# Moving a filling unit's last sums, its denominators and the cut of the V transfers around two layer changes

## The chip, the cores and the metric

The kernel runs on one core of one Trainium2 chip. The metric is the device time of one execution in microseconds (us). The kernel before was timed three times: 2504.41, 2506.2 and 2507.76 us, so its median is 2506.2 us.

## The reference, cut to what matters

Four layers run one after another on an activation `x` of two batch rows with 512 channels: attention, token mixer, attention, token mixer. Each is added to its input.

```python
q = (x @ wq).reshape(B, Sq, Hq, Dh).transpose(0, 2, 1, 3)      # Hq = 32, Dh = 128
k = jnp.repeat(k_cache, 4, axis=1)                             # 8 kv heads, 32768 keys
v = jnp.repeat(v_cache, 4, axis=1)
p = softmax(einsum("bhqd,bhkd->bhqk", q, k) * Dh ** -0.5)
o = einsum("bhqk,bhkd->bhqd", p, v)
att = o.transpose(0, 2, 1, 3).reshape(B, Sq, Hq * Dh) @ wo

x = x + att(layernorm(x))
x = x + mixer(layernorm(x))    # layernorm, outer product with w1 (1792), + b1, gelu, times w2, + b2
x = x + att(layernorm(x))      # the same K and V caches again
x = x + mixer(layernorm(x))
```

Both attention layers read the whole K and V caches, 16 pairs of (batch row, kv head) with 16 MB of K and 16 MB of V each, all in float32. Each layer reads them from HBM once, 1064 MB in all with the weights, but for some cells that are kept between the layers, as told below.

## The kernel before, in words

**Units and steps.** A unit is `(layer, b, h)`: one attention layer, one batch row, one kv head with its four query heads. A unit has a K phase and a V phase. Each phase reads 64 cells; a cell is 128 partitions by 512 floats, 256 KB. Four cells are one step, so a phase has 16 steps in two halves. A K step is four matmuls into the tile `scores` (`k_step`, L335), a V step four matmuls into the tile `acc` (`v_step`, L388). The class `Order` writes out the order of all steps by hand: the K phase of a unit, then the V phase of the unit before it, and so on.

**The transfers.** One tile `mem` of 106 cells holds everything that comes from HBM. `plan_loads` decides, when the program is built, for each transfer how many cells it takes (32, 24, 16, 8 or 4, unless `Order.cut` prescribes a size), where in `mem` they lie, and after which step they are free. It reckons with its own prices, with the PE time that each hook announces (`us=`) among them, so a hook that is announced elsewhere can shift sizes and places of all later transfers. All transfers go through one queue, that of SyncE (SP, L823 for K and V, L816 for weights): it waits until the cells' last reader on TensorE is done, issues, and goes to the next; a transfer whose cells are not free holds up all behind it.

**The hooks.** Work beside the steps is hung on steps with `at(step, function, ...)` and issued behind that step in the order in which it was hung there. For a unit these are: `max_1` and `max_2` (the maximum of the scores), `turn_scores` (DVE transposes the scores, L365) and `exponentials` (ACT, L370) for each half, `denominators` (L410 to L413: sum the exponentials over the partitions, take the reciprocal `rl`), `take_out` (L419, DVE copies `acc` to the one buffer of the tile `row`), `out_1` (L427 on TensorE, the unit's heads as columns, then L442 on DVE divides them) and `out_2` (L451, the heads times `wo`, added into `rows`).

**The layer changes.** After the first attention layer the two batch rows change to the next layer one after the other. For each there are three units, `changes = ((x, fill, y), ...)`: `x` is the last unit of its batch row in layer 0, `y` the first of the same row in layer 1 (the same kv head as `x`, so all 64 V cells and 10 K cells of `x` are kept for `y`), and `fill` is a unit of the other batch row whose V phase runs while the mixer of `x`'s row is computed. So the order at a change is: V of `x`, V of `fill`, K of `y`, V of `y`. In the V phase of `fill` the hooks carry the chain of the change, one or two pieces behind each step: `out_1` and `out_2` of `x`, `take_rows`, `mix_2` (layer norm), seven pairs of Gelu tiles (`hidden_tiles`, L511 and L527), `take_rows`, `change_0` to `change_3`, at whose end the query of `y` stands in `qz` (L321). The V transfers of `fill` are cut to four cells and go through four places in `mem`; the K transfers of `y` are cut to four cells as well.

Before the change, the second half of V of `x` is cut to 16, 8, 4 and 4 cells (`TAPER`), V of the unit ahead of the first `x`, `before[-1]`, is not cut by hand, `out_1` of `fill` stands behind the first step of K of `y` and `out_2` behind the second, and its `denominators` behind the tenth step of its own V phase, which is behind the Gelu tiles:

```python
at(v0 - 1 if u == order.last else v_mid + 2, denominators, u, us=0.4)
...
late = 0 if u == order.v_before[order.last] else 1
at(v_end + late, out_1, u, us=1.2)
at(v_end + 2 * late, out_2, u, us=2.0)
...
e = v_end
at(e, out_1, u, us=1.9)
at(e + 1, out_2, u, us=2.0)
```

The last four lines are for a unit that ends its batch row in a layer, as `x` does: `e` is the end of its V phase, and all hooks of the change count from it.

Of the kernel before, what the change touches and what calls it, by code (L numbers as in the profile page):

```python
# [15 lines left out]
HALF = 32  # L16
# [24 lines left out]
class Order:  # L41


    def __init__(self, heads):
        far, f, s = list(range(heads - 2)), heads - 2, heads - 1
        self.steps = []
        self.pairs = []
        before = [(0, b, h) for h in far for b in (0, 1)] + [(0, 0, f)]
        x0, fill0, y0 = (0, 0, s), (0, 1, f), (1, 0, s)
        x1, fill1, y1, n = (0, 1, s), (1, 0, f), (1, 1, s), (1, 1, f)  # L50
        after = [(1, b, h) for h in far[:1:-1] for b in (0, 1)] + [(1, b, h) for b in (0, 1) for h in far[1::-1]]
        for i, u in enumerate(before):
            self.k(u)
            if i:
                self.v(before[i - 1])
        self.k(x0), self.v(before[-1]), self.k(fill0), self.v(x0), self.v(fill0)
        self.k(y0), self.v(y0), self.k(x1), self.k(fill1), self.v(x1), self.v(fill1)
        self.k(y1), self.v(y1), self.k(n)
        prev = n
        for u in after:  # L60
            self.k(u), self.v(prev)
            prev = u
        self.v(prev)
        self.last = prev
        self.changes = ((x0, fill0, y0), (x1, fill1, y1))
        self.units = before + [x0, fill0, y0, x1, fill1, y1, n] + after
        self.first, self.end = {}, {}
        for p, (kind, u, g) in enumerate(self.steps):
            self.first.setdefault((kind, u), p)
            self.end[kind, u, g // HALF] = p  # L70
        byv = sorted(self.units, key=lambda u: self.first["V", u])
        self.v_before = {u: byv[i - 1] if i else None for i, u in enumerate(byv)}
        self.last_of = {
            (layer, b): max((u for u in self.units if u[:2] == (layer, b)), key=lambda u: self.end["V", u, 1])
            for layer in (0, 1)
            for b in (0, 1)
        }
        self.first_of = {
            (layer, b): min((u for u in self.units if u[:2] == (layer, b)), key=lambda u: self.end["V", u, 1])
            for layer in (0, 1)  # L80
            for b in (0, 1)
        }
        self.kept = {}
        for x, _, y in self.changes:
            for g in range(KEPT_K):
                self.kept["K", x, g] = ("K", y, g)
            for g in range(KEPT_V):
                self.kept["V", x, g] = ("V", y, g)
        self.sizes = {}
        for x, fill, y in self.changes:  # L90
            self.cut("K", y, KEPT_K, (-KEPT_K % STEP,) + (STEP,) * ((2 * HALF - KEPT_K) // STEP))
            self.cut("V", x, HALF, TAPER)
            self.cut("V", fill, 0, (STEP,) * 16)
        self.cut("V", self.last, 0, (HALF // 2, HALF // 2))
        self.cut("V", self.last, HALF, FINAL)
# [100 lines left out]
def gqa_mixer_kernel(ctx: ExitStack, tc: tile.TileContext, x, kt, v, wqo, cols, out):  # L196
# [10 lines left out]
    order = Order(HKV)  # L207
# [499 lines left out]
    def at(p, f, *args, us=0.0):  # L707
        hooks.setdefault(p, []).append((f, args))
        busy[p] = busy.get(p, 0.0) + us
# [6 lines left out]
    changed = {y: (x, fill) for x, fill, y in order.changes}  # L716
# [3 lines left out]
    for u in order.units:  # L720
        layer, b, h = u
# [5 lines left out]
        us = (u, mate) if b == 0 and mate not in made and (layer == 0 or h < HKV - 2) else (u,)  # L727
# [5 lines left out]
    for name, us in users.items():  # L733
        k0 = min(first["K", u] for u in us)
        h = name if isinstance(name, int) else name[1]
        layer = min(u[0] for u in us)
        weights.append((k0 - (24 if layer == 0 else 14) if k0 else -1, (layer, h), max(end["V", u, 1] for u in us) + 3))

    for u in order.units:
        layer, b, h = u  # L740
        key = (layer, b)
        k_mid, k_end = end["K", u, 0], end["K", u, 1]
        v0, v_mid, v_end = first["V", u], end["V", u, 0], end["V", u, 1]
# [10 lines left out]
            at(p2, exponentials, u, 0, us=5.0 if p1 == p2 else 0.0)  # L754
        at(t1, turn_scores, u, 1)
        at(max(t1, p2), exponentials, u, 1)
        at(v0 - 1 if u == order.last else v_mid + 2, denominators, u, us=0.4)
        if u == order.last:
            at(v0 - 1, take_rows, key)
            at(v0 - 1, table, AF.Gelu_apprx_tanh)  # L760
# [8 lines left out]
            continue  # L769
        at(v_end, take_out, u)  # L770
        if u != order.last_of[key]:
            late = 0 if u == order.v_before[order.last] else 1
            at(v_end + late, out_1, u, us=1.2)
            at(v_end + 2 * late, out_2, u, us=2.0)
            continue
        e = v_end
        at(e - 2, mix_1, key, us=1.2)
        at(e, out_1, u, us=1.9)
        at(e + 1, out_2, u, us=2.0)
        at(e + 1, take_rows, key)  # L780
        at(e + 2, mix_2, key, us=1.2)
        if layer == 0:
# [107 lines left out]
```

## Time and profile before

| what | value |
|---|---|
| median of three runs | 2506.2 us |
| the profiled execution | 2505.56 us, its span 2503.7 us |
| HBM read | 1064.33 MB, 425 GB/s over the span |
| share of the 16 DMA engines in the K, V and weight queue | 99.0% |
| PE busy | 1380.4 us (55%) |
| DVE and ACT busy | 180.4 us and 185.9 us (7% each) |
| mean granted clock of TensorE | 0.756 |

The profile was taken on one execution; its span runs from the first to the last instruction, and 1.9 us lie around it. A row of the timeline gives the start in us, the duration, the engine, the line of the kernel, the operation with what it writes and reads, how many instructions were merged into it, and in brackets the engine's idle time ahead of it with what ended it. A float32 matmul of the program appears as two in the trace, so a step of four matmuls shows as x8. A row of the windows gives a stretch, its length, the busy time and the number of instructions of each engine, then the granted TensorE clock, the DMA share and GB/s.

### The profile page before, as it was taken

What the parts mean: (1) busy time and instruction counts of PE and PEld (TensorE: products, weight loads), DVE (VectorE), ACT (ScalarE), POOL (GpSimd) and SP (SyncE); (2) the same over time, 40 slices, a digit from 0 to 9 for tenths busy, and PEclk for the clock granted to TensorE, in tenths of its full rate; (3) what the DMA queues carried; (4) which work ended last, traced back from release to release, by engine and by line L of the source; (5) the groups of instructions that cost most, each with busy time, mean ns of one, the idle gap of its engine ahead of it and who ended that gap; (6) DMA issues with size and microseconds to landing.
All of it is one profiled execution on the core that took longest, in us unless ns stands there. A gap on an engine that the chain in (4) does not pass through costs nothing. (4 is left out here: it accounts for less than half of the span.)

```text
span 2503.7 us, 21195 instructions
## 1 busy us (share of the span) xinstructions
PE 1380.4 (55%) x9682; PEld 395.1 (16%) x9682; DVE 180.4 (7%) x487; ACT 185.9 (7%) x579; POOL 5.2 (0%) x18
## 2 busy tenths in 40 slices
PE   3455555654555545556676773555554545555567
PEld 1111111111111111111121121111111111111112
DVE  1000000000000000001010010000000000000012
ACT  0100000000000000001110101000000000000021
POOL 0000000000000000000000000000000000000000
PEclk9777776777767776778887877777777777777788
DMA  9999999999999999999999999999999999999996
GB/s 418 431 425 436 434 431 434 434 430 432 432 434 432 430 433 434 416 430 418 407 426 427 417 424 438 432 433 429 434 434 430 434 435 428 430 436 432 432 428 278
DMA packets 33651, 1065.70 MB, mean 426 GB/s; under 512 B 3989, under 2 KB 3993, under 8 KB 5146
## 3 DMA queue, kind: packets, MB, share of 16 engines
q1 hardware_dynamic: 33272, 1064.32, 99.0%
q8 instruction: 76, 1.25, 0.2%
q14 instruction: 13, 0.11, 0.0%
q10 hardware_dynamic: 290, 0.03, 0.0%
HBM read 1064.33 MB, written 0.00 MB: 425 GB/s over the span
## 5 line engine op out<-in xcount | busy, mean ns | idle before, releaser
L388 PE MATMUL acc<-mem,S 128*16 128x512 f32 x4080 | 590.7, 711 | 575.5 <-DMA mem<-in_v_dram 570.6
L335 PE MATMUL scores<-mem,qz 128*32 128x512 f32 x4096 | 602.7, 729 | 516.8 <-DMA mem<-in_kt_dram 516.7
L370 ACT ACTIVATE S<-S,neg 128x128 f32<-128x128 f32 x256 | 129.7, 509 | 2240.4 <-DVE S L365 1201.3
L335 PEld LDWEIGHTS scores<-mem,qz 128*32 128x32 f32 x4096 | 135.9, 127 | 914.5 <-issue 470.4
L388 PEld LDWEIGHTS acc<-mem,S 128*16 128x16 f32 x4080 | 124.9, 106 | 890.1 <-issue 801.4
L345 DVE TENSOR_REDUCE mx<-scores 128x1 f32<-128x512 f32 x64 | 44.2, 691 | 803.9 <-PE scores L335 796.1
L427 PEld LDWEIGHTS misc<-selg,row 128*128 128x128 f32 x256 | 48.9, 285 | 48.2 <-issue 36.8
L427 PE MATMUL misc<-selg,row 128*128 128x4 f32 x256 | 51.7, 325 | 3.3 <-DVE row L419 3.3
L365 DVE STREAM_TRANSPOSE S<-scores 128x512 f32<-128x512 f32 x64 | 45.5, 710 | 111.6 <-PE acc L388 111.6
L451 PE MATMUL rows<-mem,oT 128*1 128x512 f32 x248 | 52.5, 936 | 0.3 <-DVE oT L442 0.3
L370 ACT ACTIVATION_READ_ACCUMULATOR S<-S,neg 128x1 f32 x256 | 47.7, 186 | 0.0
L355 DVE TENSOR_REDUCE m<-misc 1x4 f32<-1x128 f32 x32 | 8.9, 279 | 379.0 <-PE misc L353 379.0
L419 DVE COPY row<-acc 128x512 f32<-128x512 f32 x32 | 22.1, 692 | 176.1 <-PE acc L388 176.1
L413 DVE RECIPROCAL rl<-misc 128x4 f32<-128x4 f32 x32 | 5.8, 183 | 360.9 <-PE misc L411 360.9
L442 DVE TENSOR_TENSOR oT<-misc,rl 128x4 f32<-128x4 f32 x32 | 5.2, 162 | 273.1 <-PE misc L427 272.6
L411 PEld LDWEIGHTS misc<-both,one 128*128 128x128 f32 x64 | 14.4, 280 | 52.7 <-issue 46.8
L300 PE MATMUL misc<-mem,xw 128*32 128x512 f32 x144 | 20.0, 618 | 1.9 <-DVE xw L276 1.9
L353 PE MATMUL misc<-ident,mxa 128*1 128x128 f32 x64 | 18.5, 387 | 2.1 <-DVE mxa L351 2.1
L307 PEld LDWEIGHTS misc<-selg,row 128*128 128x128 f32 x128 | 16.3, 199 | 17.1 <-issue 8.6
L411 PE MATMUL misc<-both,one 128*128 128x4 f32 x64 | 17.1, 338 | 3.2 <-DVE both L410 3.2
L527 ACT ACTIVATE row<-bcast,bias,scale 128x512 f32<-128x512 f32 x21 | 16.3, 778 | 31.2 <-PE rows L511 14.2
L307 PE MATMUL misc<-selg,row 128*128 128x2 f32 (+1 forms) x128 | 17.7, 260 | 0.8 <-DVE row L292 0.8
(119 smaller groups left out, 245.6 us busy)
## 6 DMA issues: line engine op xcount, KB each, us to landing
mem<-in_kt_dram SPq DMA_DIRECT2D x20, 2048.0 KB, 16.1
mem<-in_v_dram SPq DMA_DIRECT2D x37, 1024.0 KB, 8.8
mem<-in_wqo_dram SPq DMA_DIRECT2D x14, 2048.0 KB, 32.0
mem<-in_kt_dram SPq DMA_DIRECT2D x28, 1024.0 KB, 9.1
mem<-in_v_dram SPq DMA_DIRECT2D x7, 4096.0 KB, 23.6
mem<-in_v_dram SPq DMA_DIRECT2D x4, 6144.0 KB, 26.3
mem<-in_kt_dram SPq DMA_DIRECT2D x6, 4096.0 KB, 23.8
mem<-in_v_dram SPq DMA_DIRECT2D x7, 2048.0 KB, 27.1
```

What stands on the lines that cost most here:

```text
L300: nc.tensor.matmul(q_ps[us][32 * d : 32 * d + 32, :], xw[:, d, :], wq[:, d, :], start=True, stop=True)
L307: nc.tensor.matmul(pt[:, r * n : (r + 1) * n], q_row[us][:, r * DH : (r + 1) * DH], side, start=True, stop=True,)
L335: nc.tensor.matmul(sc_ps[u, half][32 * row : 32 * row + 32, :], qz[:, at : at + 32], cells(at_cell["K", u, g], 1), start=(i == 0), stop=(i ...
L345: nc.vector.tensor_reduce(mx[u][:, half : half + 1], sc_ps[u, half], axis=AX.X, op=ALU.max)
L353: nc.tensor.matmul(pm[:1, :P], mxa, ident, start=True, stop=True)
L365: nc.vector.transpose(S[half], sc_ps[u, half])
L370: nc.scalar.activation(s[:, :, h], s[:, :, h], AF.Exp, bias=neg[u][:, h : h + 1], scale=SCALE, accum_out=lsum[u][:, half, h : h + 1],)
L388: nc.tensor.matmul(acc[32 * row : 32 * row + R * QT, :], S[half][:, col : col + R * QT], vc, start=(g < NG), stop=(g >= quads - NG),)
L411: nc.tensor.matmul(pl[:, :R], ones, both, start=True, stop=True)
L419: nc.vector.tensor_copy(asb[u], acc)
L427: nc.tensor.matmul(po_of[u][:, :R], asb[u][:, t * DH : (t + 1) * DH], selg[:, t * R : (t + 1) * R], start=(t == 0), stop=(t == QT - 1 and ...
L451: nc.tensor.matmul(rows[b][32 * r : 32 * r + 1, :], oT[u][:, r : r + 1], wo_of(u)[:, r, :], start=(u == order.first_of[layer, b]), stop=(u ...
```

## The change

Five things change, and the program's list of transfers follows from them.

1. V of `before[-1]` is cut to four transfers of 16 cells. Before, the planner chose 16, 16, 24 and 8.
2. The first half of V of each `x` is cut to two transfers of 16 cells. Before, they were 24 and 8 for the first change, 8 and 24 for the second.
3. `denominators` of a `fill` unit go from behind the tenth step of its V phase to behind the fifth.
4. `out_1` and `out_2` of a `fill` unit go from behind the first and second step of K of `y` to behind the sixth and eighth step of V of `y`.
5. For both `x` units (layer 0) `out_1`, `out_2` and everything behind them in the chain of the change are hung one step later; the announced times of `out_1` and `out_2` become 1.2 and 1.1 us, in layer 1 too, where the places stay.

```diff
@@ Order.__init__
         self.sizes = {}
+        self.cut("V", before[-1], 0, (HALF // 2,) * 4)
         for x, fill, y in self.changes:
+            self.cut("V", x, 0, (HALF // 2, HALF // 2))
             self.cut("K", y, KEPT_K, (-KEPT_K % STEP,) + (STEP,) * ((2 * HALF - KEPT_K) // STEP))
@@ the hooks of a unit
-        at(v0 - 1 if u == order.last else v_mid + 2, denominators, u, us=0.4)
+        fills = [y for y, (_, fill) in changed.items() if fill == u]
+        at(v0 - 1 if u == order.last else v0 + 4 if fills else v_mid + 2, denominators, u, us=0.4)
...
-            late = 0 if u == order.v_before[order.last] else 1
+            late = 0 if u == order.v_before[order.last] else 22 if fills else 1
             at(v_end + late, out_1, u, us=1.2)
-            at(v_end + 2 * late, out_2, u, us=2.0)
+            at(v_end + (late + 2 if fills else 2 * late), out_2, u, us=2.0)
             continue
         e = v_end
         at(e - 2, mix_1, key, us=1.2)
-        at(e, out_1, u, us=1.9)
-        at(e + 1, out_2, u, us=2.0)
+        e += 1 - layer
+        at(e, out_1, u, us=1.2)
+        at(e + 1, out_2, u, us=1.1)
         at(e + 1, take_rows, key)
```

The number of instructions on PE, DVE, ACT and POOL stays. The list of transfers grows from 231 to 237: those of 4 cells from 65 to 71, of 16 from 13 to 18, while those of 8 (the weights among them) fall from 41 to 40 and those of 24 from 6 to 2; 97 of 32 cells and nine smaller ones stay. The lists differ between V of `before[-1]` and the V phase of the unit that follows the second change, and beyond that only in places in `mem`. One of these lies near the end: V of the unit `(1, 1, 1)` is placed so that its first transfer waits for the seventh K step of `(1, 1, 0)` and no longer for the sixth. The last five K transfers of each `y` now turn over three places in `mem`, where they used four.

## The prediction

> **What bounds the kernel.** I read the page first, then windows around the two changes, then the timeline there. Page:
>
> ```profile
> span 2503.7 us, 21195 instructions
> ...
> DMA  9999999999999999999999999999999999999996
> GB/s 418 431 425 436 434 431 434 434 430 432 432 434 432 430 433 434 416 430 418 407 426 427 417 424 438 432 433 429 434 434 430 434 435 428 430 436 432 432 428 278
> ...
> q1 hardware_dynamic: 33272, 1064.32, 99.0%
> ...
> mem<-in_v_dram SPq DMA_DIRECT2D x37, 1024.0 KB, 8.8
> ...
> mem<-in_kt_dram SPq DMA_DIRECT2D x28, 1024.0 KB, 9.1
> ```
>
> The DMA engines are busy in every slice but the last, and the byte count is not touched. So a part of the change moves the end only in two ways: it changes the rate at which bytes flow, or it lets the queue run dry. Work that moves between steps on PE, DVE or ACT counts only through the moment at which it frees cells. The windows (last three columns: clock, DMA share, GB/s) show how much there is to win or lose; the first row is undisturbed:
>
> ```profile
> 400.00:1000.00 600.00, 311.48 (x2122) 87.54 (x2118) 35.62 (x92) 29.54 (x112) 0.00 (x0) 0.72 1.00 432
> 1080.00:1135.00 55.00, 27.75 (x202) 7.79 (x197) 3.11 (x7) 4.22 (x16) 0.00 (x0) 0.72 0.99 424
> 1135.00:1170.00 35.00, 17.33 (x130) 4.53 (x126) 2.23 (x7) 2.11 (x8) 0.00 (x0) 0.76 0.98 422
> 1176.00:1214.00 38.00, 31.36 (x242) 11.09 (x242) 6.46 (x26) 15.84 (x27) 1.09 (x2) 0.96 1.01 421
> 1214.00:1250.00 36.00, 23.39 (x148) 4.43 (x152) 2.17 (x4) 0.00 (x0) 0.00 (x0) 0.80 0.99 397
> 1250.00:1300.00 50.00, 38.50 (x306) 11.33 (x302) 6.51 (x16) 4.14 (x16) 0.00 (x0) 0.84 1.01 426
> 1300.00:1370.00 70.00, 41.71 (x276) 10.46 (x268) 4.05 (x11) 6.34 (x24) 0.00 (x0) 0.78 1.00 427
> 1372.00:1406.00 34.00, 25.91 (x218) 8.92 (x210) 5.29 (x23) 15.72 (x27) 1.08 (x2) 1.00 1.01 419
> 1406.00:1442.00 36.00, 25.94 (x154) 4.51 (x152) 2.17 (x4) 0.00 (x0) 0.00 (x0) 0.74 1.01 418
> 1442.00:1490.00 48.00, 40.48 (x318) 12.05 (x318) 5.98 (x16) 4.14 (x16) 0.00 (x0) 0.86 1.00 420
> ```
>
> A stretch of length L at rate r loses L x (1 - r/432). V of `fill` (1176 to 1214 and 1372 to 1406) runs at about 421 with the DMA share at 1.01: that is the rate of four-cell transfers with a full queue, which the change keeps. K of `y` (1214 to 1250, 1406 to 1442) consists of the same transfers, so I take 421 as its floor too. The rest can in principle be won: 1.0 + 0.8 + 2.1 + 0.7 + 0.8 + 0.3 + 1.3 = 7.0 us.
>
> **Edits 3, 4 and 5, on PE.** Rows of the first change:
>
> ```profile
> 1201.95 0.35 PE L411 MATMUL misc<-both,one 128*128 128x4 f32 x2 [1.04 <-DVE both L410]
> ...
> 1209.35 1.05 PE L388 MATMUL acc<-mem,S 128*16 128x512 f32 x8 [0.17 <-DMA mem<-in_v_dram]
> 1210.34 1.05 PE L307 MATMUL misc<-pair,row 128*128 128x1 f32 x8
> 1211.42 0.16 DVE L321 COPY qz<-misc 128x4 f32<-128x4 f32 x1 [1.80 <-PE misc L307]
> 1211.83 1.05 PE L388 MATMUL acc<-mem,S 128*16 128x512 f32 x8
> 1214.33 1.05 PE L388 MATMUL acc<-mem,S 128*16 128x512 f32 x8 [1.45 <-DMA mem<-in_v_dram]
> 1216.26 1.06 PE L427 MATMUL misc<-selg,row 128*128 128x4 f32 x8
> 1218.13 1.04 PE L451 MATMUL rows<-mem,oT 128*1 128x512 f32 x8
> 1222.22 1.07 PE L335 MATMUL scores<-mem,qz 128*32 128x512 f32 x8 [1.33 <-DMA mem<-in_kt_dram]
> 1256.56 10.29 PE L388 MATMUL acc<-mem,S 128*16 128x512 f32 x80 [2.40 <-ACT S L370]
> 1289.55 0.64 PE L335 MATMUL scores<-mem,qz 128*32 128x512 f32 x4 [2.82 <-DMA mem<-in_kt_dram]
> ```
>
> The denominators (edit 3) free PE of a 1.04 us wait for DVE behind the Gelu tiles, once per change. The V steps that follow wait for DMA again (0.17, then 1.45 us), so this is worth 0; without that cover it would be a gain of 1.0 us per change. Behind the fifth step nothing new waits: the exponentials end ahead of the Gelu table.
>
> The chain of the change (edit 5) comes one step later. `change_3` stood between the V steps of 1209.35 and 1211.83; now it stands behind the latter: 1211.83 + 1.05 + 1.05 + 0.16 puts `qz` at 1214.1. K of `y` needs it only behind the last V step, 1214.33 + 1.05 = 1215.4, which waits for DMA anyway. I take 0; the margin is 1.3 us, so a chain later by a whole V step (2.5 us) would start K of `y` 1.2 us late, and the ends are 0 and +1.2 per change.
>
> The heads of `fill` (edit 4) are 1.06 + 1.04 = 2.1 us of PE. They leave a phase in which PE waits for DMA (1.33 us at 1222.22) and enter one in which PE runs without a gap from 1256.56 on and frees the cells for the next K. Everything behind V of `y` on PE comes 2.1 us later, and so does the release of the cells of its last eight steps. Cover: SP has them issued well ahead (DMA share 1.01 in 1250 to 1300), and PE has caught up by 1289.55, where it waits 2.82 us. I take 0; without cover it is +2.1 per change.
>
> **Edits 1 and 2, and the size of transfers.** The new list has six more transfers of four cells than the 28 + 37 of the page. Six of them are 6.29 MB: at 421 GB/s 14.94 us, at 432 14.56 us. **+0.4 us**; ends 0 (rate of large ones) and +1.3 (at the 397 of K of `y`). Swapping 24 and 8 for 16 and 16 has rates of 427 and 432 around it: 0.
>
> V of `before[-1]` in 16s frees the next unit's K cells earlier. The transfer that was issued just in time there is that of 1092.51:
>
> ```profile
> 1092.51 0.33 SPq L823 DMA_DIRECT2D mem<-in_kt_dram  x1
> ...
> 1086.00:1098.00 12.00, 7.45 (x46) 1.91 (x50) 0.18 (x1) 0.00 (x0) 0.00 (x0) 0.59 1.04 431
> ```
>
> Over 12 us the rate is still 431, so hardly anything was lost; the whole stretch 1080 to 1135 lost 1.0. I take **-0.3**, ends -1.0 and 0. V of `x` arrives earlier in parts, but its last four cells come behind the same bytes, so the chain of the change starts when it did.
>
> **The list that follows.** In K of `y` the last five transfers now turn over three places, not four. A place is free when its K step is done:
>
> ```profile
> 1232.02 1.93 PE L335 MATMUL scores<-mem,qz 128*32 128x512 f32 x8 [0.55 <-DMA mem<-in_kt_dram]
> ...
> 1234.02 0.33 SPq L823 DMA_DIRECT2D mem<-in_kt_dram  x1
> 1244.19 0.80 SPq L823 DMA_DIRECT2D mem<-in_kt_dram  x2
> ...
> DMA to landing us min/median/max: 5.4/26.9/45.6
> ...
> DMA to landing us min/median/max: 7.2/8.5/8.8
> ...
> 1244.00:1246.00 2.00, 1.49 (x12) 0.20 (x8) 0.00 (x0) 0.00 (x0) 0.00 (x0) 0.50 0.68 188
> ```
>
> From the start of a step to the next issue it is 2.0 us (1232.02 to 1234.02, at half clock). From issue to landing the shortest of the kernel is 5.4 us; in V of `fill` (1177 to 1206, the second landing row) 7.2, but there transfers queue behind others. So a round takes about 7.4 us. Three places hold 3 x 1.049 MB / 421 GB/s = 7.47 us of work: just enough. Before, one transfer per change stood in this way, the one issued at 1244.19, and the two us around it ran at 188 GB/s, a loss of 1.1 us. I take +0.4 per change for more of this, **+0.8**; ends 0 and the 1.1 again per change, +2.3.
>
> The rest of the list between the changes has small shifts in both directions. K behind V of `y` now comes in 8s, each waiting for another V step; 1250 to 1300 lost only 0.7, so I take **-0.3**, ends -0.7 and +0.5. The first 16 cells of V of the second `x` wait for the eighth K step of its `fill`:
>
> ```profile
> 1309.39 1.92 PE L335 MATMUL scores<-mem,qz 128*32 128x512 f32 x16 [1.57 <-DMA mem<-in_kt_dram]
> ```
>
> That step is done at 1311.3, while 32 more cells of K of `fill` are still to be moved, 19.6 us at the 427 GB/s of that stretch: 0.
>
> Near the end, the first V transfer of `(1, 1, 1)` waits for one K step more:
>
> ```profile
> 2400.93 0.33 SPq L823 DMA_DIRECT2D mem<-in_v_dram  x1
> 2401.43 1.03 PE L335 MATMUL scores<-mem,qz 128*32 128x512 f32 x6
> 2402.99 1.03 PE L335 MATMUL scores<-mem,qz 128*32 128x512 f32 x6
> 2402.00:2410.00 8.00, 5.76 (x50) 1.47 (x44) 0.69 (x1) 3.68 (x6) 0.00 (x0) 0.79 0.98 401
> ```
>
> The K steps among the last Gelu tiles follow at 1.56 us, so it is issued 1.6 us later, where the queue already ran thin (401 GB/s over 8 us). **+0.3**; ends 0 and +1.6.
>
> **Sum:** 0.4 - 0.3 + 0.8 - 0.3 + 0.3 = +0.9 us on the profiled execution's 2505.56 us: **2506.5 us**. The median of the runs is 0.6 us above that execution; from it the sum would be 2507.1. The kernel before spreads over 3.3 us, and a measurement can tell about 0.2% from no change, 5.0 us.
>
> **A fixed price per transfer.** The 4-cell transfers follow each other at 1.049 MB / 421 GB/s = 2.49 us, of which the bytes at 432 take 2.43; with a full queue a transfer costs 0.06 us of its own. A rule speaks against the change here: the Trainium skill, page "DMA: Bandwidth & Descriptors", section "Anatomy of one DMA — SWDGE (gpsimd) path", fits a fixed 2.0 us per transfer plus its bytes over 436 GB/s. By that, if the fixed part stood in the queue, the six more transfers would cost 12 us where I put 0.4, and the sum would be 2518.1; the trace's 2.49 us disagrees.
>
> **The rivals.**
> - Slower, the round of three places doesn't close. If a landing takes the 7.2 us seen in V of `fill`, a round is 9.2 us, 3.07 per transfer against 2.49: 0.58 x 5 = 2.9 us per change, 5.8 for both, in place of my 0.8: 2511.5. It decides once issue to landing exceeds 5.5 us with nothing queued ahead. For it: the 188 GB/s at 1244. Against: 7.2 us contains a queue. Less PE work in K of `y` may also bring half clock earlier (0.50 in that row), which makes the 2.0 us sure.
> - Faster, the new list closes the thin stretches. Half of the 7.0 us won is 2502.1; all of it 2498.6. For it: the releases come earlier around the first `x`. Against: share 0.98 to 1.01 in nearly all rows, so most of the loss is no idleness.
> - No effect, the queue never notices: 2505.6.
> - Slower, each further transfer stands alone. The shortest landing is 5.4 us, 2.4 of them bytes; if the other 3.0 us were paid in the queue, six more transfers give +18, 2524.1 in place of my 0.4. Against: the 2.49 us above. It decides once a transfer costs over 0.8 us of its own.
>
> **How the numbers follow.** Forecast, with the case of no effect in it (2503.5 to 2509): 0.68. The faster case 0.17, of which 0.06 beyond 0.2% under the median (2501.2). The slower round 0.12, of which 0.06 above 2511.2. Transfers that stand alone, or a stall that I haven't seen, 0.03. So faster 0.06, same 0.85, slower 0.09. The range 2502.3 to 2510.5 reaches half into both rivals; outside it stay about 0.09 below and 0.10 above.
>
> **What would show it.** K of `y` at 390 to 421 GB/s in both changes; V of `fill` at 420; no PE wait for DVE at L411; L427 and L451 inside V of `y`, followed by a wait for K no longer than 2.82 us. Wrong if K of `y` runs under 380 GB/s, if SP waits on PE with the DMA share under 0.9 for more than 3 us behind V of `y`, or if the part before 1080 us moves.

## The result and the profile after

The changed kernel takes 2508.76 us, the median of 20 runs (2505.01 to 2513.21); the kernel before, timed beside it, 2506.14 us, the median of 20 runs (2503.55 to 2508.93). The medians differ by 2.6 us. The ratio on record, which is not that of the medians, is 1.0015 with a 95% interval of 1.0008 to 1.0022, or 2.0 to 5.5 us: a small but real loss. The forecast was 2506.5 us, with a range of 2502.3 to 2510.5. The sign and the range held; the sum of +0.9 us was too small.

The profiled execution of the changed kernel took 2508.48 us. Its page (span, the main DMA queue, the chain that ended last, the four-cell K transfers):

```profile
span 2506.6 us, 21206 instructions
...
q1 hardware_dynamic: 34136, 1064.32, 99.0%
...
DMA 75%; PE 24%; issue 0%; ACT 0%; DVE 0%; SPq 0%; POOLq 0%
...
mem<-in_kt_dram SPq DMA_DIRECT2D x34, 1024.0 KB, 8.3
```

The bytes are the same 1064.32 MB and the queue is as busy as before. Six more K transfers have four cells. Windows of the changed kernel around the two layer changes (the last three columns are clock, DMA share and GB/s):

```profile
1080.00:1135.00 55.00, 25.87 (x162) 6.62 (x154) 3.11 (x7) 4.22 (x16) 0.00 (x0) 0.75 1.00 427
1135.00:1170.00 35.00, 24.54 (x154) 6.17 (x158) 2.23 (x7) 2.11 (x8) 0.00 (x0) 0.74 0.99 426
1172.00:1214.00 42.00, 33.34 (x279) 11.31 (x271) 6.60 (x25) 15.84 (x27) 1.09 (x2) 1.00 1.01 420
1214.00:1250.00 36.00, 23.91 (x133) 3.48 (x133) 2.17 (x4) 0.00 (x0) 0.00 (x0) 0.72 1.00 396
1250.00:1300.00 50.00, 40.86 (x336) 12.84 (x336) 6.86 (x18) 4.14 (x16) 0.00 (x0) 0.90 1.01 423
1372.00:1406.00 34.00, 26.50 (x224) 8.76 (x216) 4.94 (x21) 15.58 (x27) 0.78 (x2) 1.00 1.01 420
1406.00:1442.00 36.00, 25.05 (x147) 4.29 (x146) 2.52 (x6) 0.00 (x0) 0.31 (x1) 0.74 1.02 409
1442.00:1490.00 48.00, 40.88 (x330) 13.13 (x330) 6.15 (x17) 4.13 (x16) 0.00 (x0) 0.89 0.99 415
```

K of the first `y` (1214 to 1250) ran at 397 before and runs at 396, so by this window the two executions are equally thin. K of the second `y` (1406 to 1442) fell from 418 to 409 and the stretch behind it from 420 to 415: 36 x 9/432 + 48 x 5/432 = 1.3 us. V of `fill` is unchanged at 420. V of `before[-1]` (1080 to 1170) improved from 424 and 422 to 427 and 426, which is 0.7 us. But its transfers are issued from 1037 us on, and 1040 to 1080 fell from 408 to 401, which is 0.6 us lost. Over both stretches the rate is the same in the kernel before and in the changed kernel:

```profile
1040.00:1170.00 130.00, 62.90 (x444) 17.10 (x448) 6.62 (x18) 6.33 (x24) 0.00 (x0) 0.72 0.98 419
1040.00:1170.00 130.00, 67.70 (x432) 17.37 (x436) 6.63 (x18) 6.33 (x24) 0.00 (x0) 0.73 0.98 419
```

A single pair of executions does not carry a verdict of 2.6 us; that is what the experiments are for.

The steps of K of the first `y` show more than its window. Here are rows of PE in the changed kernel, and the row in which SP issues the transfer for the step at 1245.22; then two steps of the same phase in `e3_ring`, a kernel told of below in which these transfers go round four places:

```profile
1235.88 1.93 PE L337 MATMUL scores<-mem,qz 128*32 128x512 f32 x8 [1.39 <-DMA mem<-in_kt_dram]
1237.87 0.33 SPq L827 DMA_DIRECT2D mem<-in_kt_dram  x1
1238.43 1.94 PE L337 MATMUL scores<-mem,qz 128*32 128x512 f32 x8 [0.62 <-DMA mem<-in_kt_dram]
1241.42 1.93 PE L337 MATMUL scores<-mem,qz 128*32 128x512 f32 x8 [1.05 <-DMA mem<-in_kt_dram]
1245.22 1.93 PE L337 MATMUL scores<-mem,qz 128*32 128x512 f32 x8 [1.87 <-DMA mem<-in_kt_dram]
```

```profile
1243.13 1.94 PE L356 MATMUL scores<-mem,qz 128*32 128x512 f32 x8 [1.42 <-DMA mem<-in_kt_dram]
1245.61 1.94 PE L356 MATMUL scores<-mem,qz 128*32 128x512 f32 x8 [0.55 <-DMA mem<-in_kt_dram]
```

SP issues 2.0 us behind the start of the step that frees the place (1235.88), and the step that uses the transfer starts at 1245.22: one round of three steps takes 9.3 us. With four places the steps follow one another at 2.48 us, three of them in 7.4 us; here two of them come 2.99 and 3.80 us apart. The kernel before is as thin over the window for another reason: its one transfer that waits for the step three back is the one at 1244.19, with 188 GB/s around it.

The DMA share, 1.00 in this window, does not show the loss. The median packet of 8 KB takes 0.31 us; in K of the first `y` 41 of 1640 such packets take more than 0.6 us, the longest 2.16 us, against 1 of 1686 in `e6_four` below, in which no transfer of `y` waits for the step three back. So the share counts as busy some time in which few bytes flow.

The timeline of the changed kernel at the first change, with the moved work in it (L413 denominators, L309 and L323 the end of the chain, L429 and L453 the heads of `fill`):

```profile
1189.18 0.39 PE L413 MATMUL misc<-both,one 128*128 128x4 f32 x2
1189.94 1.05 PE L390 MATMUL acc<-mem,S 128*16 128x512 f32 x8 [0.38 <-DMA mem<-in_v_dram]
...
1213.27 1.05 PE L309 MATMUL misc<-pair,row 128*128 128x1 f32 x8
1214.36 0.16 DVE L323 COPY qz<-misc 128x4 f32<-128x4 f32 x1 [1.78 <-PE misc L309]
1214.79 1.05 PE L390 MATMUL acc<-mem,S 128*16 128x512 f32 x8
1215.66 3.92 PE L337 MATMUL scores<-mem,qz 128*32 128x512 f32 x32
...
1263.11 1.05 PE L429 MATMUL misc<-selg,row 128*128 128x4 f32 x8
1265.82 1.04 PE L453 MATMUL rows<-mem,oT 128*1 128x512 f32 x8
...
1291.01 1.92 PE L337 MATMUL scores<-mem,qz 128*32 128x512 f32 x16 [0.84 <-DMA mem<-in_kt_dram]
1295.99 2.50 PE L337 MATMUL scores<-mem,qz 128*32 128x512 f32 x16 [3.06 <-DMA mem<-in_kt_dram]
```

The denominators wait for nothing; the V step behind them waits for DMA. `qz` stands at 1214.5, ahead of the last V step, and K of `y` follows that step without a gap. The heads stand inside V of `y`, and PE has caught up with the transfers by 1291.

### The profile page after: what moved, and what is told of

It is laid out like the page before. It is cut to its first block, busy times and chain, and to the rows that moved or that the text cites. A ratio compares the mean times of both kernels' runs of the same rounds, so it can differ in the third digit from the quotient of the medians.

```text
span 2506.6 us, 21206 instructions
## 1 busy us (share of the span) xinstructions
PE 1394.1 (56%) x9682; PEld 396.8 (16%) x9682; DVE 180.4 (7%) x487; ACT 185.8 (7%) x579; POOL 5.2 (0%) x18
## 3 DMA queue, kind: packets, MB, share of 16 engines
q1 hardware_dynamic: 34136, 1064.32, 99.0%
## 4 chain that ended last, share of the span: by engine, by line
DMA 75%; PE 24%; issue 0%; ACT 0%; DVE 0%; SPq 0%; POOLq 0%
DMA mem<-in_v_dram 38%; DMA mem<-in_kt_dram 38%; PE acc L390 11%; PE scores L337 11%; PE misc L309 1%; PE misc L413 0%; PE rows L674 0%; ACT S L372 0%; PE misc L429 0%; PE rows L453 0%; DVE mx L347 0%; ACT mem L684 0%; ACT mem L696 0%; PE rows L513 0%; PE bcast L649 0%
## 5 line engine op out<-in xcount | busy, mean ns | idle before, releaser
L390 PE MATMUL acc<-mem,S 128*16 128x512 f32 x4080 | 600.6, 723 | 558.5 <-DMA mem<-in_v_dram 552.2
L429 PEld LDWEIGHTS misc<-selg,row 128*128 128x128 f32 x256 | 48.9, 285 | 46.3 <-issue 39.4
L429 PE MATMUL misc<-selg,row 128*128 128x4 f32 x256 | 51.7, 325 | 1.6 <-DVE row L421 1.6
L453 PE MATMUL rows<-mem,oT 128*1 128x512 f32 x248 | 49.8, 891 | 0.3 <-DVE oT L444 0.3
L413 PEld LDWEIGHTS misc<-both,one 128*128 128x128 f32 x64 | 13.8, 269 | 49.2 <-issue 44.5
L309 PEld LDWEIGHTS misc<-selg,row 128*128 128x128 f32 x128 | 16.3, 199 | 18.4 <-issue 8.5
L309 PE MATMUL misc<-selg,row 128*128 128x2 f32 (+1 forms) x128 | 17.7, 260 | 0.8 <-DVE row L294 0.8
L413 PE MATMUL misc<-both,one 128*128 128x4 f32 x64 | 16.6, 330 | 2.0 <-DVE both L412 2.0
```

The costliest lines, as they stand in the source:

```text
L309: nc.tensor.matmul(pt[:, r * n : (r + 1) * n], q_row[us][:, r * DH : (r + 1) * DH], side, start=True, stop=True,)
L390: nc.tensor.matmul(acc[32 * row : 32 * row + R * QT, :], S[half][:, col : col + R * QT], vc, start=(g < NG), stop=(g >= quads - NG),)
L413: nc.tensor.matmul(pl[:, :R], ones, both, start=True, stop=True)
L429: nc.tensor.matmul(po_of[u][:, :R], asb[u][:, t * DH : (t + 1) * DH], selg[:, t * R : (t + 1) * R], start=(t == 0), stop=(t == QT - 1 and ...
L453: nc.tensor.matmul(rows[b][32 * r : 32 * r + 1, :], oT[u][:, r : r + 1], wo_of(u)[:, r, :], start=(u == order.first_of[layer, b]), stop=(u ...
```

## The experiments

The changed kernel has two halves that can be separated: where the hooks stand, and the list of transfers that follows. My theory was that the hooks are free and that the list costs a little, most of it through the last five K transfers of each `y`, which go round three places in `mem` instead of four. One rival said that this round is far too short (+5.8 us for both changes). Others were a cost of the hooks themselves and a price for each further transfer. The runs of before beside each kernel have medians of 2505.1 to 2506.0 us; ratios are against those. Where a difference of ratios is given in us, it is that difference times 2506 us; the medians can give 1 to 2 us more or less.

In the first two kernels a table `ANNOUNCED` (34 steps, only its use is shown) gives the planner the other kernel's announced PE times, so that it makes the other kernel's list cell for cell.

### The new list without the moved hooks, and the moved hooks without the new list

```diff
 # e1_list, against the kernel before
+        self.cut("V", before[-1], 0, (HALF // 2,) * 4)
         for x, fill, y in self.changes:
+            self.cut("V", x, 0, (HALF // 2, HALF // 2))
...
+    for p, us in ANNOUNCED.items():
+        busy[p] = busy.get(p, 0.0) + us
     loads = plan_loads(order, weights, busy)
```

> The hooks of before with the changed kernel's list of transfers: the two cuts, and the planner is told the changed announced times while the hooks themselves stay. If the list of transfers makes the 2.6 us (my theory: the last K transfers of y over three places, and more transfers that are issued just in time), this runs 1.5 to 4 us over before, about 2508.5. If the moved hooks make it (rival 1), it runs within 0.7 us of before. If the six more small transfers alone make it (rival 2), it is also some 2 us slower, and only the ring experiment tells the two apart.

```diff
 # e2_hooks, against the changed kernel
-        self.cut("V", before[-1], 0, (HALF // 2,) * 4)
         for x, fill, y in self.changes:
-            self.cut("V", x, 0, (HALF // 2, HALF // 2))
...
+    for p, us in ANNOUNCED.items():
+        busy[p] = busy.get(p, 0.0) - us
     loads = plan_loads(order, weights, busy)
```

> The hooks of the changed kernel (heads of fill in V of y, denominators among the Gelu tiles, chain one step later) with the list of transfers of before, cell for cell. My theory: within 0.7 us of before, because the moved PE work frees no cell that the queue is waiting for. Rival 1, the hooks cost it: 2 to 3 us over before. If hooks and list each cost only in company, both this and the list alone are near before.

The new list alone: 2511.32 us, ratio 1.0022 [1.0013, 1.0030], 5.4 us over before by the medians, where I expected 1.5 to 4; it is slower than the whole change too, but the intervals overlap. The hooks alone: 2507.05 us, 1.0006 [0.9997, 1.0015], not told apart from no change, though 1.2 us over before by the medians where I expected 0.7 at most. So the list alone is enough for the loss, and for the hooks none is shown. Windows of the new list alone:

```profile
1214.00:1250.00 36.00, 23.07 (x140) 4.38 (x144) 2.17 (x4) 0.00 (x0) 0.00 (x0) 0.72 0.99 376
1406.00:1442.00 36.00, 25.16 (x164) 5.50 (x162) 2.71 (x8) 0.00 (x0) 0.52 (x1) 0.81 0.99 399
```

K of both `y` is thin, 376 and 399 GB/s. With the hooks of before, two more pieces (the heads of `fill`) stand between these K steps; that they make this kernel the slower one is not shown.

### The round of places, taken away and put in

`replaced` takes the finished list, gives named transfers another place in `mem` and works out anew after which step each may start. Nothing else moves.

```diff
 # e3_ring, against the changed kernel: four places
     loads = plan_loads(order, weights, busy)
+    places = {}
+    for _, _, y in order.changes:
+        places.update({("K", y, 44): 90, ("K", y, 48): 102, ("K", y, 52): 98, ("K", y, 56): 94, ("K", y, 60): 102})
+    loads = replaced(order, loads, weights, places)
```

> The changed kernel, but the last five K transfers of each y turn over four places as in before (cells 90, 102, 98, 94, 102), nothing else. My theory, the round of three places: K of y comes back to the rate of before or above it and the time falls by 1 to 2 us, to 2506.5 to 2508. Rival 2 (number and place of the other transfers): it stays within 0.7 us of the changed kernel's 2508.8.

Measured 2506.28 us, 1.0006 [0.9997, 1.0014]: 0.0009 of the 0.0015 are gone. The interval overlaps that of the change, so this run alone does not settle it. As in the kernel before, the last of the five transfers still waits for the step three back. Its windows:

```profile
1214.00:1250.00 36.00, 25.38 (x139) 3.45 (x138) 2.17 (x4) 0.00 (x0) 0.00 (x0) 0.72 1.02 420
1250.00:1300.00 50.00, 41.53 (x344) 13.22 (x344) 6.87 (x18) 4.13 (x16) 0.00 (x0) 0.91 1.00 421
1406.00:1442.00 36.00, 23.95 (x145) 3.94 (x144) 2.17 (x4) 0.00 (x0) 0.00 (x0) 0.80 0.98 394
1442.00:1490.00 48.00, 39.92 (x330) 12.96 (x326) 6.95 (x19) 4.13 (x16) 0.00 (x0) 0.90 1.01 428
```

K of the first `y` is back at 420. K of the second is not (394), but what follows it runs at 428 in place of 415, so over both stretches nothing is lost against the changed kernel: -36 x 15/432 + 48 x 13/432 = +0.2 us. In this execution the gain is in the first change.

```diff
 # e8_list_four: the kernel e1_list with the same five places as e3_ring
```

> The hooks of before, the changed kernel's list, and the last five K transfers of each y over four places: the list alone less its round of three. If the round is all of the list's cost: within 0.8 us of before, 2505.5 to 2506.7, some 4 to 5 us under the list alone. If the rest of the list (sizes, number, places) has a share with these hooks: 1.5 to 3 us over before.

Measured 2507.10 us, 1.0007 [0.9998, 1.0016], against 1.0022 with three places: 0.0015, or 3.8 us, are gone, and the intervals of the two kernels hardly touch. What is left, 1.8 us, lies where I had put a share of the rest of the list; its interval includes none. K of the second `y` is as thin here (392) as in `e3_ring`.

```diff
 # e5_three, against the kernel before: three places
+    places = {}
+    for _, _, y in order.changes:
+        places.update({("K", y, 44): 102, ("K", y, 48): 98, ("K", y, 52): 94, ("K", y, 56): 102, ("K", y, 60): 98})
+    (x1, _, _) = order.changes[1]
+    places.update({("K", x1, 10): 90, ("K", x1, 30): 98})
+    loads = replaced(order, loads, weights, places)
```

> The kernel before, with its hooks and transfers, but the last five K transfers of each y over three places (102, 98, 94); the pieces of K behind them move to the free place, same sizes. If the round of three is the cause and enough alone: 1.5 to 3.5 us over before, like the changed kernel or a little under it, 2507.5 to 2509.5. If it needs the rest of the changed list: within 0.7 us of before.

Measured 2508.71 us against 2505.13, 1.0016 [1.0007, 1.0025]. This is the kernel before in everything but these places, and it loses as much as the whole change does. Its windows:

```profile
1214.00:1250.00 36.00, 22.82 (x144) 4.34 (x144) 2.17 (x4) 0.00 (x0) 0.00 (x0) 0.79 1.00 390
1250.00:1300.00 50.00, 38.86 (x302) 11.30 (x302) 6.52 (x16) 4.14 (x16) 0.00 (x0) 0.84 1.00 416
1406.00:1442.00 36.00, 26.73 (x171) 6.19 (x174) 3.87 (x15) 0.42 (x1) 0.55 (x1) 0.78 1.00 392
```

Against the 397, 426 and 418 of before that is 36 x 7/432 + 50 x 10/432 + 36 x 26/432 = 3.9 us; the medians differ by 3.6. The profiled execution took 2511.41 us, 2.7 above its median, and V of the second `fill`, whose places are not touched, was thin in it too (405 against 419, 1.1 us), so the two figures agree only roughly. The round of three places is sufficient for the loss (e5, whose interval lies above 1), and its removal takes most of it away (e8; e3 points the same way).

```diff
 # e6_four, against the kernel before: no transfer of y on three places
+    places = {("K", y, 60): 90 for _, _, y in order.changes}
+    loads = replaced(order, loads, weights, places)
```

> The kernel before, but the last K transfer of each y, the only one that waited for a step just three transfers back, goes to the place of the one four back (90). If each such transfer costs about a fifth of what the changed kernel lost per change, this runs 0.5 to 1 us under before, 2505 to 2505.5, and the two us at 188 GB/s near 1244 are gone. If those were paid back elsewhere: within 0.3 us of before.

```profile
1214.00:1250.00 36.00, 22.88 (x156) 4.40 (x152) 2.17 (x4) 0.00 (x0) 0.00 (x0) 0.86 1.02 423
1406.00:1442.00 36.00, 25.19 (x157) 4.47 (x159) 2.17 (x4) 0.00 (x0) 0.00 (x0) 0.76 1.02 420
```

K of both `y` ran at 420 or more in the profiled execution, but the time is 2505.53 us, 0.9997 [0.9988, 1.0005]. One transfer per change on three places is worth less than this measurement resolves. The rates are clearer than the times. In the four profiled kernels in which no transfer of `y` waits for the step three back (this one, e10, e11 and e12) K of `y` runs at 420 to 424 in all eight windows. Where the last one waits so (before, e2, e3, e8) it runs at 392 to 420, and where five do (the changed kernel, e1, e5 and the first change of e4) at 376 to 409.

### Two places, to see how long a round is

```diff
 # e7_two, against the changed kernel
+    for _, _, y in order.changes:
+        places.update({("K", y, 44): 102, ("K", y, 48): 98, ("K", y, 52): 102, ("K", y, 56): 98, ("K", y, 60): 102})
```

> The changed kernel, but the last three K transfers of each y over two places, so that each waits for the step two transfers back. By the round that the runs with three places show (about 2.0 us from step to issue and 7.2 from issue to landing, 9.2 in all) two places give 4.6 us per transfer against 3.1 over three: 1.5 us more for three transfers, 4.6 per change, 9 us in all, so 2517 to 2519. If the last transfers aren't on the path that sets the end, it stays within 1.5 us of the changed kernel.

Measured 2513.75 us, 1.0033 [1.0021, 1.0045]. The sign is right, the size is about half of what I expected. The reason is in the landing times. Here is the time from issue to landing of the K transfers in flight at the end of K of the first `y` (shortest, median, longest), in the kernel with two places, then in the changed kernel (three), then in the changed kernel with `LAND_US = 3.2`, told of below (four):

```profile
DMA to landing us min/median/max: 4.6/5.7/15.9
```

```profile
DMA to landing us min/median/max: 6.7/7.3/11.3
```

```profile
DMA to landing us min/median/max: 7.9/8.8/13.2
```

A landing is no constant: with fewer places fewer transfers queue ahead, and it shrinks. The shortest, 4.6 us, has little ahead: it is issued at 1247.81, and the transfer before it lands 1.1 us later. With the 2.0 us from the start of a step to the next issue, I estimate the shortest round at 6.6 us. Two places hold 2 x 2.49 = 5.0 us of transfers, so by this estimate each transfer loses (6.6 - 5.0)/2 = 0.8 us. The last K steps of the first `y` bear it out: they start at 1242.10, 1245.81, 1248.94 and 1252.49, two rounds of 6.8 and 6.7 us. The time agrees roughly: 0.0018 more than for the changed kernel, 4.5 us, or 0.75 us for each of the six transfers that came to two places, but with some 3.5 us of uncertainty, and the changed kernel loses on these transfers too. I had put the long landing into the round of two as well, and so expected twice as much.

Three places hold 7.5 us, so with the shortest landing the round would close with 0.9 us to spare. In the changed kernel it did not: the rounds that end at 1245.22, 1247.73 and 1250.19 took 9.3, 9.3 and 8.8 us, with landings of 7.3, 7.3 and 6.7 us. Why these landings stayed so long although transfers came late is not shown. Four places hold 10.0 us.

### The change without its cuts

```diff
 # e4_nocut, against the changed kernel
-        self.cut("V", before[-1], 0, (HALF // 2,) * 4)
         for x, fill, y in self.changes:
-            self.cut("V", x, 0, (HALF // 2, HALF // 2))
```

> The changed kernel without its two cuts (V of before[-1] and V of x in 16s); the planner then makes another list, in which V of the second fill and all of K of the second y turn over three places (84, 80, 76), and the last five K transfers of the first y over three too. My theory: a round of three places is at the edge, so this has about 30 transfers at the edge where the changed kernel has 10, and runs 3 to 8 us over before, 2509 to 2514; the second change shows the lower rate. If a round of three places closes (against my theory), it runs like the changed kernel or better, 2506 to 2509.

Measured 2514.93 us, 1.0043 [1.0031, 1.0055], the slowest of all and a little above my range. Without the cuts the planner puts V of the second `fill` and most of K of the second `y` on three places:

```profile
1372.00:1406.00 34.00, 24.13 (x210) 7.93 (x210) 4.34 (x14) 15.25 (x26) 0.54 (x1) 1.00 1.00 381
1406.00:1442.00 36.00, 23.97 (x140) 5.38 (x136) 3.71 (x14) 0.60 (x1) 0.54 (x1) 0.72 0.96 364
```

Against 420 and 409 that is 34 x 39/432 + 36 x 45/432 = 6.8 us; the ratios differ by 0.0028, 7.0 us. So with three places even V of `fill`, which runs at 420 in the changed kernel, falls to 381; PE has the Gelu tiles to do there as well. The two cuts therefore pay under the moved hooks (1.0015 against 1.0043): with them the list keeps V of the second `fill` on four places.

### Fewer kept cells, and a planner that knows the landing

`plan_loads` chooses places with a landing of its own reckoning, `LAND_US = 1.1`, which it counts from the end of the transfer's bytes. By its prices a four-cell transfer with nothing ahead lands 4 x 0.6024 + 0.12 + 1.1 = 3.6 us after its start; the shortest landing above is 4.6 us. (The medians of 5.7 to 8.8 us also hold what queues ahead, which the planner counts apart.) The next kernels change one or two constants.

```diff
 # e9_kept8, against the kernel before
-KEPT_K = 10
+KEPT_K = 8
```

> The kernel before with KEPT_K = 8 in place of 10: eight K groups stay in SBUF instead of ten, no K transfer is of two cells any more, the list has 219 transfers where it had more, and four cells (1.05 MB) are moved in addition. In y only the transfers of g56 and g60 are left on a round of three places. If a short round costs where it stands, the loss at g16 (about 1.7 us per change of layer, 3.4 us in all) goes and the added bytes cost about 2.4 us at 432 GB/s: 2503.5 to 2505.5 us, ratio 0.999 to 1.000. If the rounds are not what costs and only bytes count: 2507.5 to 2508.5 us, ratio 1.001.

Measured 2511.35 us, 1.0023 [1.0014, 1.0032]: both of my cases were too low. This list has two transfers in each `y` that wait for the step three back, one more than the kernel before, and K of `y` runs at 405 and 406. The loss has another place, behind K of the second `y`. Window and timeline of this kernel, then the window of the kernel before:

```profile
1450.00:1458.00 8.00, 7.79 (x52) 1.76 (x56) 0.00 (x0) 2.19 (x10) 0.00 (x0) 0.69 0.61 211
```

```profile
1445.33 0.33 SPq L816 DMA_DIRECT2D mem<-in_wqo_dram  x1
1455.38 5.48 SPq L823 DMA_DIRECT2D mem<-in_kt_dram  x3
```

```profile
1450.00:1458.00 8.00, 8.00 (x60) 1.82 (x56) 0.00 (x0) 1.54 (x7) 0.00 (x0) 0.74 0.98 373
```

SP issues a weight transfer at 1445.33 and nothing more until 1455.38, because the cells of the next K transfer come free only with the third V step of `y`; the queue runs dry, 8 x (1 - 211/373) = 3.5 us. The list was drawn up for another number of kept cells and got a hole that I had not looked for.

```diff
 # e10_kept8_land, against the kernel before
-KEPT_K = 10
+KEPT_K = 8
...
-LAND_US = 1.1
+LAND_US = 2.2
```

> As the run with KEPT_K = 8, and the planner is told a longer landing (LAND_US = 2.2), so that it gives every K transfer of both y a round of four places; the list has 239 transfers. Theory of the short rounds: no place is late in either change of layer, K of y runs at 420 GB/s or more throughout, and the 20 added small transfers cost about 0.06 us each: 2503.5 to 2506 us, ratio 0.999 to 1.000. Rival (three places were enough in the kernel before, the two transfers on three places cost nothing): this run is slower than the one with KEPT_K = 8 alone by the 20 small transfers, 1 to 1.5 us, and shows no higher rate in K of y.

Measured 2504.78 us, 0.9997 [0.9988, 1.0006], with K of `y` at:

```profile
1214.00:1250.00 36.00, 24.01 (x152) 4.28 (x144) 2.17 (x4) 0.00 (x0) 0.00 (x0) 0.78 1.02 424
1406.00:1442.00 36.00, 22.25 (x148) 4.19 (x144) 2.17 (x4) 0.00 (x0) 0.00 (x0) 0.86 1.02 423
```

This is 6.6 us under the same kernel with the short landing, although it has 20 transfers more. About half of that is the hole behind K of the second `y`, which is gone: 1442 to 1490 runs at 419 against 389, 3.3 us.

```diff
 # e11_land, against the changed kernel; e12_before_land, the same against the kernel before
-LAND_US = 1.1
+LAND_US = 3.2
```

> The changed kernel with the planner told LAND_US = 3.2, so that step to issue and issue to landing together (9.2 us) are what the trace shows; it keeps four places for the last transfers of both y by itself, and the list has 261 transfers. Theory of the short rounds: K of y loses nothing to places, but the list is cut smaller elsewhere: 2506.3 to 2508 us, ratio 1.0000 to 1.0007, below the changed kernel's 2508.8. Rival (the count of transfers, not the rounds, sets the time): 2509.5 us or more, ratio above 1.0013.

> The kernel before with nothing but LAND_US = 3.2: its list is cut for rounds of four places as that of the changed kernel with LAND_US = 3.2 (2503.3 us), with the same 261 transfers; the two differ in where V and the heads and denominators stand. If the gain of that run over the changed kernel came from the rounds, and moving the heads and denominators costs and brings nothing: 2503.0 to 2504.5 us, ratio 0.9988 to 0.9995, and its runs lie within 1 to 2 us of one another (the kernel before spreads over 7 us). If the changed placing gains something of its own that the short rounds had hidden: 2504.5 to 2506 us, ratio 0.9995 to 1.0000. If it costs something of its own: 2501 to 2503 us, ratio below 0.9988.

The changed kernel with the longer landing takes 2503.34 us (2503.10 to 2504.01 over 11 runs), 0.9992 [0.9983, 1.0001] of the kernel before. The changed kernel itself, timed in another measurement, never came under 2505.01 in 20 runs, so the 5.4 us between the medians come from that constant, the only line in which the two kernels differ. The kernel before with it takes 2503.64 us (2502.92 to 2505.30), 0.9989 [0.9980, 0.9998]. Windows of the changed kernel with `LAND_US = 3.2`, then of the kernel before with it, then one of the kernel before:

```profile
1214.00:1250.00 36.00, 22.79 (x136) 3.13 (x128) 2.36 (x4) 0.00 (x0) 0.00 (x0) 0.78 1.02 424
1406.00:1442.00 36.00, 23.79 (x138) 3.29 (x136) 2.77 (x5) 0.00 (x0) 0.00 (x0) 0.76 1.02 422
```

```profile
60.00:120.00 60.00, 28.82 (x196) 8.46 (x200) 2.42 (x7) 4.24 (x16) 0.00 (x0) 0.66 1.01 436
1172.00:1214.00 42.00, 33.38 (x258) 10.90 (x262) 6.77 (x26) 15.86 (x27) 1.09 (x2) 0.96 1.00 410
1214.00:1250.00 36.00, 23.82 (x149) 4.32 (x142) 3.01 (x6) 0.00 (x0) 0.00 (x0) 0.79 1.01 422
1406.00:1442.00 36.00, 24.59 (x152) 4.46 (x152) 2.70 (x5) 0.00 (x0) 0.00 (x0) 0.77 1.02 422
```

```profile
60.00:120.00 60.00, 29.32 (x208) 8.49 (x208) 3.49 (x9) 4.56 (x17) 0.00 (x0) 0.74 0.99 421
```

K of both `y` is at 422 to 424 in both. The longer landing also changes a place that I had never looked at, the second unit of the kernel: 436 GB/s in place of 421 over 60 us, 2.1 us, in both kernels that have it. Not all of that lasts. The V step that waits for DMA at 132.26 us in the kernel before starts 1.3 us earlier in both, but the one at 1075.92 only 0.7 and 0.8 us earlier. So this explains less than 1 us of the 3 us by which the changed kernel with the longer landing came out under what I expected; the rest is not located. V of the first `fill` is thinner in the kernel before with the longer landing (410 against 421 GB/s, 42 x 11/432 = 1.1 us); what thins it is not shown.

These two kernels also answer the question about the change itself. Each has 261 transfers and no K transfer at the end of `y` on three places. They differ in the hooks and the cuts, and their medians differ by 0.3 us, well inside either interval. With enough places the change is worth nothing measurable in either direction. The kernel before with `LAND_US = 3.2` is the one version whose interval lies wholly under the kernel before.

## Why the prediction was right, and where its sum was off

- **The bytes bind, and moved work counts only through the cells it frees: right.** The queue is at 99.0% before and after, the chain that ended last in the changed kernel is 75% DMA, and the hooks alone cost nothing that can be told (1.0006 [0.9997, 1.0015]).
- **Edit 3, the denominators, 0: right.** The wait of 1.04 us for DVE is gone and the V steps wait for DMA, 0.38 us behind it and about 1.0 us at the steps that follow.
- **Edit 5, the chain one step later, 0: right.** `qz` stands at 1214.5 against 1214.1 forecast, still ahead of the end of V at 1215.8.
- **Edit 4, the heads of `fill`, 0: right within what the runs tell.** PE has caught up by 1291, but the longest wait for K behind the heads is 3.06 us where I named 2.82 as the bound, and the stretch is thinner (423 against 426 GB/s, 0.3 us; 421 with four places, so it isn't the short round).
- **Six more small transfers, +0.4: borne out in kind.** The kernel before with 30 more transfers than its own 231 is faster, not slower, so a transfer in a full queue costs little of its own; the single term was never measured by itself. The Trainium skill's page "DMA: Bandwidth & Descriptors", section "Anatomy of one DMA — SWDGE (gpsimd) path", puts a fixed 2.0 us on each transfer that goes by gpsimd; the transfers here are issued by SyncE. As an estimate from that figure, 30 more would have cost 60 us if the fixed part stood in the queue, and the runs disagree with that reading. In the landing they agree: the page's fit gives an estimated 2.0 + 2.4 = 4.4 us for a transfer with nothing ahead, and the shortest landing with two places is 4.6 us.
- **V of `before[-1]` in 16s, -0.3: within its ends, but no gain is shown.** What 1080 to 1170 gains, 0.7 us, is lost from 1040 to 1080; over both the rate is 419 before and after. The forecast looked only at the later stretch.
- **The round of three places, +0.8: the step that was mis-sized.** By the runs it is about 2.3 us in the changed kernel (1.0015 to 1.0006 with four places), 3.8 under the hooks of before (1.0022 to 1.0007) and 3.6 when put into the kernel before alone. I took the shortest landing of the kernel, 5.4 us, called 7.4 against 7.47 "just enough", and priced it as a matter of a few steps. In the changed kernel the landings in this round were 6.7 to 7.3 us and the round 8.8 to 9.3. The slower rival had the right mechanism, and its round of 9.2 us is the one that the trace shows, but its price of 5.8 us was too high: the five steps behind 1235.88 took 14.31 us where those of `e3_ring` took 12.41, so 1.9 us in the first change against the rival's 2.9. It also took 7.2 us of landing as fixed, and e7 shows that it shrinks to 4.6 when fewer transfers queue ahead. The truth lay between the two, and so did the time.
- **The rest of the list, -0.3: wrong in sign in this pair of executions.** 1250 to 1300 and 1442 to 1490 lost 3 and 5 GB/s, 0.9 us in the profiled execution, beyond the end of +0.5, where I had hoped for K in 8s to fill them. With four places (e3) the first stays thin, 421, and the second rises to 428; what thins the first stays open.
- **Near the end, +0.3: no cost seen.** The K step that waits for DMA at 2387.47 in the kernel before starts at 2390.22 in the changed kernel, 2.75 us later, and the span ends 2.9 us later. So in this pair at most 0.2 us arise behind it. No run measured this step alone.
- **The signs named.** K of `y` at 396 and 409 and V of `fill` at 420 are as named, and the first 1080 us run at 430 GB/s before and after. The wait for K of 3.06 us is over the bound. Behind V of the second `y` the DMA share was 0.81 for 3 us (1454 to 1457), at the edge of the sign for being wrong.

The interval of the change is 1.8 us to either side, so the terms of 0.3 and 0.4 us are below what its time can test. Their sum came near the time because the one large term had the right sign; that the small ones are right is not shown by it.

What is left of the change with four places, 1.0006 and 1.0007 in e3 and e8, isn't resolved from zero by any run; the pair with the longer landing says that it is small.

## What to carry to other kernels

In a kernel bound by one DMA queue that issues just in time, count how many bytes lie between the step that frees a place and the transfer that takes it: they must cover step, issue and landing with room to spare. Here three places of 1 MB (7.5 us) were too few for a round that I estimate at 6.6 us at its shortest and that took 8.8 to 9.3 us, and K of `y` lost nothing that shows where all its transfers had four (10.0 us). A planner that places buffers should be given the landing that the trace shows, counted as the planner counts it, since an edit that only moves small work can make it choose a shorter round elsewhere. An edit list should be read for this distance at every transfer, not only where the edit stands.

## What the runs showed of the hardware that was not expected

- From issue to landing a 1 MB transfer took 5.7, 7.3 and 8.8 us (medians at the end of K of the first `y`) with two, three and four places in turn; in the second change 6.1 us with three and 8.7 with four. 4.6 us was the shortest.
- In a stretch in which transfers came late, the DMA share stayed at 1.00 while 396 GB/s flowed, because single packets of 8 KB took up to 2.16 us in place of 0.31. Only the rate showed the loss.
- The spread of a kernel's runs goes with its slack: 2505.01 to 2513.21 us for the changed kernel (20 runs), 2503.10 to 2504.01 for the same with the longer landing (11 runs). The kernel before with the longer landing spreads over 2.4 us and e10 over 1.8. But e3, e6 and e8, with four places in `y` and the short landing elsewhere, still spread over 4 to 5 us, so the round in `y` alone does not make the spread, and what does is not shown.
- A list with more and smaller transfers was the faster one: 261 at 2503.64 us against 231 at 2505.98 us. The list with 261 also has the longer rounds, so this shows that the pieces cost little, not that they gain.
